# Order of weight preparation and accumulator banks at the seam between the last MLP and the token-mixing stage

## Chip, cores and metric

One core of one Trainium2 chip (TensorE = PE with its weight loads PEld, VectorE = DVE, ScalarE = ACT, GpSimd = POOL, SyncE = SP). The time is the device time of one execution in microseconds, the median over runs, as printed in the table below.

## What is computed

Four sequences of 768 tokens, 8 heads of 48, pass through three layers. The reference, cut to what matters:

```
# gated linear attention, per head:
state = f[t] * state + k[t] v[t]^T ;  y[t] = q[t] state         (f = sigmoid(f_logit))
# layer 2, x is [4, 768, 384]:
h = x^T @ U @ V ;  u = x + h^T
x = u + relu(u @ w_ch1) @ w_ch2                                  # 384 -> 1536 -> 384
# layer 3:
theta = x @ w_theta
y = w_tok_r @ (x * cos(theta)) + w_tok_i @ (x * sin(theta))      # 768 x 768 over tokens
u = x + y
out = u + relu(u @ w_ch)
```

## The kernel before

Activations lie with channels on the 128 partitions, so a batch is `xT[b]`, three blocks of 128 channels by 768 tokens. Every fp32 product is done with both operands split into a high and a low part (`split`: ACT copies the high part, L135, POOL subtracts for the low one, L132), as three products hi x hi, lo x hi, hi x lo. Weights come as 64-bit floats and are turned into fp32 on the chip (`fetch`): a DMA on the SP queue into a buffer of a ring, two ACT scalings (L863, L865: `scale`), two DVE instructions (L868, L871: `join`), then the split. So a piece of weights has four steps, called load, scale, join and store here. The ring for the weights of the last layer has four buffers; a buffer is free for the next load when POOL has done the subtraction of the piece that was in it.

The kernel has three stretches: attention of batch 0; three MLPs of layer 2 (batches 0 to 2) with the attention of the next batch laced in; the MLP of batch 3, called the last MLP, with the preparation of layer 3 laced in; then layer 3 for the four batches, called the next stage.

*The MLP* (`moe1`) goes in groups of four of the 12 blocks of hidden channels, for one half of the tokens after the other (six groups in the last MLP, 24 blocks in all). A piece is nine matmuls of 128 x 128 weights on 384 tokens. `w1g` (L477) forms a hidden block in bank A3 or A4; ACT takes the relu as high part hh (L482), DVE the low part hl (L483). `w2g` (L493 with hh, L496 with hl) adds it into three accumulators in banks A0, A1 and A2. When a group's last block is in, DVE adds the accumulators to `xT` (L500). The list alternates: w1g of block n, then w2g of block n - 1. The first six of the last MLP's 48 pieces go ahead of the stretch that this is about; 42 remain (`m3[6:]`).

*The next stage* works in units of 128 tokens, six to a batch, counted from 0. For a unit, `theta` has five parts: `prep` splits the 128 columns (POOL x2lo), `tr` transposes them into bank B1 (L586, ACT copies x2tok, L588), `mmt` multiplies by w_theta into bank B0 (nine matmuls, L598) and reduces the angle on DVE (kk and r, L602 to L606) and takes two sines on ACT (sh, sn, L609, L610), `trig` forms z = x cos, x sin on DVE (L619 to L622) and copies the high part zh on ACT (L623), `rest` subtracts the low part zl on POOL. `tok` has six pieces of six matmuls (L646) that add the unit's share into all six banks A0 to A5, in the order of the banks. The theta parts run two units ahead of `tok`: units 0 and 1 are prepared during the last MLP (a list called `pre`), unit n + 2 between the `tok` pieces of unit n. From the second batch on, the output product (`chan`, L674, banks B0 and B1) of the batch before is laced in too.

*The order.* The engines take instructions in program order, and the program's order is written by hand. Each list is of (cost, function) pairs. `merge` gives each item of a side list a place in a stretch of the main list by its cost, `place` by a position of its own: a step at position x of a main list stands ahead of the first piece whose middle lies behind x of the list's total cost. Before the change the weight pieces pass through `staged` and `tok_weights`: one item of a side list does the scaling of piece i + 1, the join of piece i, the store of piece i - 1 and the load of the piece three further on, all at one place. The six pieces of w_theta and w_ch lie by `CWA` in the first 0.3 of the last MLP, and 20 of the 30 items of the token weights' list by `M3` in the rest. The other ten are run one at a time, three in each unit of the next stage (`cv`). Loads of the token weights overwrite the tiles `W` of MLP weights that are no longer needed (`WMAP`).

## Time and profile before

| | us |
|---|---|
| median of 3 runs (lowest to highest) | 732.85 (732.4 to 736.12) |
| the profiled execution | 735.42 |
| its span from first to last instruction | 733.6 |
| PE busy in the span | 696.8 (95%) |
| DVE, ACT, POOL busy | 463.2 (63%), 290.2 (40%), 317.6 (43%) |

A profile row shows one execution. Times in it count from the start of the span. A row of a timeline may merge several instructions of one kind (x6); its second number is then their length together. PE's matmuls overlap, so the pitch from start to start says more than the length of one. "idle before <-" names what ended the idle time of the engine. An ACT, DVE or POOL row that waits holds up everything behind it on its engine.

### The profile page before, as it was taken

Reading aid. Unit: us, or ns where it says so; the run is one execution under the profiler, and the core shown is the slowest. Engines: PE = TensorE matmul, PEld = TensorE weight load, DVE = VectorE, ACT = ScalarE, POOL = GpSimd, SP = SyncE. Lnnn points to the kernel's source line nnn. Section 1 sums busy time; section 2 is a strip of 40 time slices with the busy share of each in tenths; the row PEclk is TensorE's granted clock in tenths of the full one; section 3 lists DMA queues with packets and bytes.
Section 4 is the critical chain, followed back from the end, with each engine's and each line's share of the span. In section 5 each row is a group of like instructions: output and inputs, shape, how many; then the busy total and the mean of one; then the engine's idle time right before and its main releaser. Section 6 shows DMA issues by size and latency. Waiting matters only on the chain.

```text
span 733.6 us, 12972 instructions
## 1 busy us (share of the span) xinstructions
PE 696.8 (95%) x5221; PEld 655.9 (89%) x5221; DVE 463.2 (63%) x705; ACT 290.2 (40%) x613; POOL 317.6 (43%) x338
## 2 busy tenths in 40 slices
PE   7988899999999999999999999898899999999996
PEld 6766798999899999899989999898799999999996
DVE  8795778666544545544433578779786569459433
ACT  1577474533332224333323466555442233233211
POOL 5586657542443333342432144335555245336212
PEclk9799899999999999999999999999899999999999
DMA  9795253322122222122000243333000000000102
GB/s 176 172 267 133 68 156 75 55 42 49 44 44 45 44 45 43 45 44 44 2 2 1 87 140 104 102 108 109 0 1 22 33 13 11 33 22 1 44 21 70
DMA packets 17956, 46.14 MB, mean 63 GB/s; under 512 B 2272, under 2 KB 8544, under 8 KB 17888
## 3 DMA queue, kind: packets, MB, share of 16 engines
q1 hardware_dynamic: 15760, 39.13, 21.7%
q10 hardware_dynamic: 2128, 6.10, 3.1%
q8 instruction: 43, 0.70, 0.4%
q14 instruction: 25, 0.20, 0.1%
HBM read 40.50 MB, written 4.72 MB: 62 GB/s over the span
## 4 chain that ended last, share of the span: by engine, by line
PE 39%; DVE 12%; ACT 4%; issue 2%; POOL 2%; DMA 1%; DVEq 0%; POOLq 0%; ACTq 0%
PE ps_A L646 12%; PE ps_A L477 7%; PE ps_B L674 5%; PE ps_A L493 5%; PE ps_B L598 3%; PE ps_A L496 2%; DVE r L606 1%; DVE r L605 1%; DVE kk L603 1%; DVE z L622 1%; DVE z L621 1%; DVE sh L619 1%; DVE r L604 1%; DVE kk L602 1%; DVE r L871 1%
## 5 line engine op out<-in xcount | busy, mean ns | idle before, releaser
L483 DVE SCALAR_TENSOR_TENSOR hl<-ps_A,hh 128x384 fp32r<-128x384 f32 x96 | 53.1, 554 | 151.5 <-ACT hh L482 151.3
L646 PE MATMUL ps_A<-W,zh 128*128 128x384 f32 x576 | 126.1, 340 | 4.2 <-ACT zh L623 3.9
L493 PE MATMUL ps_A<-hh,W 128*128 128x384 f32 x576 | 122.1, 347 | 4.1 <-DVE xT L500 2.9
L477 PE MATMUL ps_A<-uh,W 128*128 128x384 f32 x576 | 121.3, 345 | 1.7 <-ACT uh L444 1.7
L493 PEld LDWEIGHTS ps_A<-hh,W 128*128 128x128 f32 x576 | 100.5, 191 | 8.0 <-ACT r L865 2.9
L646 PEld LDWEIGHTS ps_A<-W,zh 128*128 128x128 f32 x576 | 101.1, 189 | 5.1 <-ACT zh L623 4.5
L477 PEld LDWEIGHTS ps_A<-uh,W 128*128 128x128 f32 x576 | 100.0, 190 | 4.8 <-ACT uh L444 2.5
L482 ACT ACTIVATE hh<-ps_A 128x384 fp32r<-128x384 f32 x96 | 46.9, 489 | 140.0 <-PE ps_A L477 139.1
L132 POOL TENSOR_TENSOR zl<-z,zh 128x768 fp32r<-128x768 f32 x24 | 44.8, 1866 | 102.1 <-ACT zh L623 92.6
L220 DVE RECIPROCAL f<-p 112x128 f32<-112x128 f32 x96 | 87.0, 930 | 0.7
L646 PE MATMUL ps_A<-W,zl 128*128 128x384 f32 x288 | 74.3, 339 | 1.9 <-POOL zl L132 1.9
L132 POOL TENSOR_TENSOR ul<-xT,uh 128x384 fp32r<-128x384 f32 x45 | 49.8, 1115 | 52.9 <-ACT uh L444 35.7
L223 POOL TENSOR_TENSOR raw<-raw,f 112x256 f32<-112x256 f32 x48 | 37.5, 782 | 76.4 <-DVE f L220 61.8
L477 PE MATMUL ps_A<-ul,W 128*128 128x384 f32 x288 | 66.9, 338 | 0.6 <-POOL ul L132 0.6
L496 PE MATMUL ps_A<-hl,W 128*128 128x384 f32 x288 | 66.0, 337 | 0.0
L213 POOL TENSOR_TENSOR raw<-raw,p 112x512 f32<-112x512 f32 x24 | 30.9, 1287 | 66.1 <-DVE p L209 54.1
L646 PEld LDWEIGHTS ps_A<-W,zl 128*128 128x128 f32 x288 | 52.5, 190 | 2.5 <-POOL zl L132 2.5
L477 PEld LDWEIGHTS ps_A<-ul,W 128*128 128x128 f32 x288 | 51.9, 189 | 1.6 <-POOL ul L132 1.6
L496 PEld LDWEIGHTS ps_A<-hl,W 128*128 128x128 f32 x288 | 52.0, 190 | 0.0
L609 ACT ACTIVATE sh<-r 128x384 f32<-128x384 f32 x24 | 12.6, 526 | 85.6 <-DVE r L606 85.6
L132 POOL TENSOR_TENSOR W<-r,W 128x384 fp32r<-128x384 f32 x24 | 27.5, 1148 | 42.0 <-ACT W L135 42.0
L602 DVE TENSOR_SCALAR kk<-ps_B 128x384 f32<-128x384 f32 x24 | 13.3, 554 | 43.7 <-PE ps_B L598 43.7
(161 smaller groups left out, 1255.2 us busy)
## 6 DMA issues: line engine op xcount, KB each, us to landing
raw<-in_qkf_dram SPq DMA_DIRECT2D x41, 288.0 KB, 5.2
r<-in_wtok_dram SPq DMA_DIRECT2D x24, 384.0 KB, 3.2
vt<-in_v_dram SPq DMA_DIRECT2D x24, 192.0 KB, 5.4
out_dram<-o SPq DMA_DIRECT2D x24, 192.0 KB, 1.9
xT<-in_w_dram SPq DMA_DIRECT2D x5, 768.0 KB, 4.8
w<-in_w_dram ACTq DMA_DIRECT2D x4, 768.0 KB, 6.9
w<-in_w_dram SPq DMA_DIRECT2D x2, 768.0 KB, 8.2
raw<-in_qkf_dram ACTq DMA_DIRECT2D x5, 288.0 KB, 5.6
```

The source lines that it names most:

```text
L132: eng.tensor_tensor(out=out_, in0=a, in1=b, op=ALU.subtract)
L213: nc.gpsimd.tensor_tensor(out=x, in0=x, in1=p, op=ALU.mult)
L220: nc.vector.reciprocal(out=f[:, j], in_=p[:, j])
L223: nc.gpsimd.tensor_tensor(out=x, in0=x, in1=f[:, j - 1:j + 1], op=ALU.mult)
L477: mm(out=t, lhsT=w1t(lo, fb)[:, k, 128 * fo:128 * fo + 128], rhs=x[:, k], start=(n == 0), stop=(n == 8))
L482: nc.scalar.activation(out=hh, in_=t, func=ACTF.Relu)
L483: nc.vector.scalar_tensor_tensor(out=hl, in0=t, scalar=0.0, in1=f32(hh), op0=ALU.max, op1=ALU.subtract)
L493: mm(out=st["acc"][k], lhsT=w2t(lo, fb)[:, fo, 128 * k:128 * k + 128], rhs=hh, start=(first_of(f) and lo == 0), stop=False)
L496: mm(out=st["acc"][k], lhsT=w2t(0, fb)[:, fo, 128 * k:128 * k + 128], rhs=hl, start=False, stop=last_of(f))
L598: mm(out=t, lhsT=x[:, k], rhs=w[:, k], start=(n == 0), stop=(n == 8))
L646: mm(out=t, lhsT=z[:, i, 128 * k:128 * k + 128], rhs=w[:, S * i + HT * th:S * i + HT * th + HT], start=(s == 0 and n == 0), stop=(s == NCH ...
L674: mm(out=t, lhsT=w[:, k, 128 * m:128 * m + 128], rhs=x[:, k], start=(n == 0), stop=(n == 8))
```

## The change

In the last MLP, the groups' accumulators alternate between banks A0, A1, A2 and banks A5, B0, A2, and the adds into `xT` go in the order A2 first. The theta products of the first two units use bank B1. The 30 pieces of the last layer's weights (w_theta, w_ch, token weights, in this order) get a ring of four tiles, and each of their four steps gets a position of its own, in `NPOS`: below 1.0 in the last MLP, above 1.0 in the first batch of the next stage. The 11 parts of the theta list for units 0 to 2 get positions too (`PPOS`). `place` puts them into the two lists. `staged`, `tok_weights`, `cv` and the constants of their lanes go.

```diff
--- before.py
+++ after.py
@@ -33,9 +33,39 @@
 WARM = 28
 KEEP = (15, 1, 1, 1, 1, 1, 0, 3, 16, 0)
 NPRE = 6
-N3 = 20
-CWA = 0.101
-M3 = ((0.333, 0.867), (0.3, 0.999))
+NPOS = (
+    (0.0241, 0.0644, 0.0738, 0.0988),
+    (0.0327, 0.1266, 0.1466, 0.1716),
+    (0.0387, 0.0965, 0.1019, 0.1953),
+    (0.1482, 0.1974, 0.1982, 0.257),
+    (0.1717, 0.2209, 0.2217, 0.2574),
+    (0.2218, 0.2763, 0.2771, 0.3021),
+    (0.1961, 0.2721, 0.2921, 0.3444),
+    (0.2578, 0.3057, 0.3257, 0.3448),
+    (0.2686, 0.3245, 0.3378, 0.4217),
+    (0.3157, 0.3892, 0.4092, 0.4392),
+    (0.3464, 0.4224, 0.4402, 0.4629),
+    (0.4081, 0.4783, 0.504, 0.5388),
+    (0.4758, 0.5558, 0.5758, 0.6037),
+    (0.4694, 0.5765, 0.5881, 0.6181),
+    (0.5027, 0.5727, 0.5927, 0.659),
+    (0.5472, 0.6172, 0.6372, 0.7129),
+    (0.6045, 0.66, 0.6639, 0.7498),
+    (0.6206, 0.664, 0.684, 0.7502),
+    (0.6796, 0.7552, 0.7696, 0.9267),
+    (0.7599, 0.7662, 0.8484, 0.9399),
+    (0.7555, 0.8704, 0.8712, 0.9403),
+    (0.8292, 0.8974, 0.9192, 0.9746),
+    (0.9315, 0.9828, 0.9928, 1.022),
+    (0.9407, 0.9937, 1.004, 1.124),
+    (0.9525, 0.9978, 1.008, 1.188),
+    (1.001, 1.002, 1.096, 1.205),
+    (1.047, 1.07, 1.12, 1.412),
+    (1.126, 1.206, 1.256, 1.412),
+    (1.269, 1.369, 1.419, 1.525),
+    (1.33, 1.361, 1.48, 1.64),
+)
+PPOS = (0.3588, 0.3882, 0.428, 0.4924, 0.4929, 0.5759, 0.5869, 0.7626, 0.7666, 0.8224, 0.8643)
 W0 = (100, 1200, 800, 600)
 
@@ -486,7 +516,8 @@
         def w2g(th, f):
             hh, hl = st.pop(("h", th, f))
             if first_of(f):
-                st["acc"] = [ps(f"A{k}", [128, HT]) for k in range(NK)]
+                two = b == B - 1 and order.index((th, f)) % 2
+                st["acc"] = [ps(t, [128, HT]) for t in (("A5", "B0", "A2") if two else ("A0", "A1", "A2"))]
             fb, fo = divmod(f, 4)
             for k in range(NK):
                 for lo in range(2):
@@ -495,10 +526,12 @@
             for k in range(NK):
                 mm(out=st["acc"][k], lhsT=w2t(0, fb)[:, fo, 128 * k:128 * k + 128], rhs=hl,
                    start=False, stop=last_of(f))
-                if last_of(f):
+            if last_of(f):
+                for k in (2, 0, 1) if b == B - 1 else range(NK):
                     u = xT[b][:, k, HT * th:HT * th + HT]
                     nc.vector.tensor_tensor(out=u, in0=st["acc"][k], in1=u, op=ALU.add)
 
+        order = [(th, o) for o in range(0, NF, span) for th in range(2)]
         todo = [(th, f) for o in range(0, NF, span) for th in range(2) for f in range(o, o + span)]
         for n, a in enumerate(todo):
             L.append((1470, lambda a=a: w1g(*a)))
@@ -511,63 +544,43 @@
     thw = {}
 
     def weights_2(pool):
-        L = []
-
-        def issue(nm, src, i):
+
+        ring = [pool.tile([128, 768], I32, name=f"r64_{i}") for i in range(4)]
+
+        def issue(n, src):
+            return fetch(nc, pool, src, [128, 384], nc.sync, buf=ring[n % 4])
+
+        def dst(nm, i):
+            if nm in ("th", "ch"):
+                if i == 0:
+                    thw[nm] = [pool.tile([128, NK, DM], F32R, name=nm + x) for x in ("hi", "lo")]
+                return [t[:, i] for t in thw[nm]]
             if i == 0:
-                thw[nm] = (pool.tile([128, NK, DM], F32R, name=nm + "hi"), pool.tile([128, NK, DM], F32R, name=nm + "lo"))
-            return fetch(nc, pool, src[:, 384 * i:384 * i + 384], [128, 384], nc.sync, "r64", bufs=4)
+                st["tok", nm] = [wtile(k) for k in WMAP[nm]]
+            return [t[:, 384 * i:384 * i + 384] for t in st["tok", nm]]
 
         def store(nm, i, w):
-            hi, lo = thw[nm]
-            split(hi[:, i], lo[:, i], w, lo_eng=nc.gpsimd)
-
-        for nm, src in (("th", wth), ("ch", wch)):
-            for i in range(NK):
-                L.append((lambda nm=nm, src=src, i=i: issue(nm, src, i), lambda w, nm=nm, i=i: store(nm, i, w)))
-        return staged(L, 4)
-
-    def staged(L, ahead, delay=1, lag=1):
-
-        got, out = {}, [(0, lambda i=i: got.update({i: L[i][0]()})) for i in range(min(ahead, len(L)))]
-
-        def step(i):
-            if i + 1 < len(L):
-                got[i + 1][0]()
-            if i < len(L):
+            split(*dst(nm, i), w, lo_eng=nc.gpsimd)
+
+        tok_ = [(s, i, wtok[s]) for s in range(NCH) for i in range(4)]
+        order = [("th", i, wth) for i in range(NK)] + [("ch", i, wch) for i in range(NK)] + tok_
+        return steps_of([(lambda n=n, src=src, i=i: issue(n, src[:, 384 * i:384 * i + 384]),
+                          lambda w, nm=nm, i=i: store(nm, i, w)) for n, (nm, i, src) in enumerate(order)])
+
+    def steps_of(L):
+
+        got = {}
+
+        def one(i):
+            def load():
+                got[i] = L[i][0]()
+
+            def join():
                 got[i] = got[i][1]()
-            if i >= lag:
-                L[i - lag][1](got.pop(i - lag))
-            j = i - max(lag, delay) + ahead
-            if i >= max(lag, delay) and j < len(L):
-                got[j] = L[j][0]()
-
-        out.append((0, lambda: got[0][0]()))
-        out += [(1000, lambda i=i: step(i)) for i in range(len(L) + lag)]
-        return out
-
-    def tok_weights(pool):
-        L = []
-        ring = []
-
-        def issue(n):
-            if n == 0:
-                ring.extend(pool.tile([128, 384, 2], I32, tag="r64", bufs=4, name="r64") for _ in range(4))
-            s, i = divmod(n, 4)
-            return fetch(nc, pool, wtok[s, :, 384 * i:384 * i + 384], [128, 384], nc.sync,
-                         buf=ring[n % 4].rearrange("p n t -> p (n t)"))
-
-        def store(n, w):
-            s, i = divmod(n, 4)
-            if i == 0:
-                st["tok", s] = wtile(WMAP[s][0]), wtile(WMAP[s][1])
-            hi, lo = st["tok", s]
-            sl = slice(384 * i, 384 * i + 384)
-            split(hi[:, sl], lo[:, sl], w, lo_eng=nc.gpsimd)
-
-        for n in range(4 * NCH):
-            L.append((lambda n=n: issue(n), lambda w, n=n: store(n, w)))
-        return staged(L, 4, lag=1)
+
+            return load, lambda: got[i][0](), join, lambda: L[i][1](got.pop(i))
+
+        return [one(i) for i in range(len(L))]
 
     WMAP = {0: (6, 7), 1: (0, 1), 2: (8, 9), 3: (2, 3), 4: (10, 11), 5: (4, 5)}
 
@@ -591,7 +604,7 @@
         def mmt():
             hi, lo = st.pop(("x2", b, s))
             wh, wl = thw["th"]
-            t = ps("B0", [128, DM])
+            t = ps("B0" if (b, s) > (0, 1) else "B1", [128, DM])
             n = 0
             for (x, w) in ((hi, wh), (hi, wl), (lo, wh)):
                 for k in range(NK):
@@ -791,40 +804,25 @@
         p2 = fast.enter_context(tc.tile_pool(name="st2", bufs=1))
         units = [(b, s) for b in range(B) for s in range(NCH)]
         th = [theta(p2, *u) for u in units]
-        pre = [(330, th[0][0]), (330, th[0][1]), (1470, th[0][2]), (500, th[0][3]), (900, th[0][4]),
-               (330, th[1][0]), (330, th[1][1]), (1470, th[1][2]), (500, th[1][3]), (900, th[1][4]),
-               (0, th[2][0])]
-        tw = tok_weights(p2)
-        cw = weights_2(p2)
-        merge(m3[6:], (0.0, 0.0, cw[:4]), (CWA, 0.3, cw[4:]), (*M3[0], pre), (*M3[1], tw[:N3]))
-        tw = tw[N3:]
+        pre = [th[0][0], th[0][1], th[0][2], th[0][3], th[0][4], th[1][0], th[1][1], th[1][2], th[1][3], th[1][4], th[2][0]]
+        timed = [list(zip(PPOS, pre)), []]
+        for fs, at in zip(weights_2(p2), NPOS):
+            for f, x in zip(fs, at):
+                timed[x >= 1.0].append((x % 1.0, f))
+        place(m3[6:], timed[0])
         nop = lambda: None
+        main = []
         for n, (b, s) in enumerate(units):
             _, tr, mmt, trig, rest = th[n + 2] if n + 2 < len(units) else [nop] * 5
             prep = th[n + 3][0] if n + 3 < len(units) else nop
             cl = [f for _, f in chan(p2, b - 1)[2 * s - 2:2 * s]] if b and s in (1, 2, 3) else [nop] * 2
             tk = [f for _, f in tok(b, s)]
-
-            def cv():
-                run(tw[:1])
-                del tw[:1]
-
-            tk[0]()
-            prep()
-            tr()
-            cv()
-            tk[1]()
-            mmt()
-            cv()
-            tk[2]()
-            cl[0]()
-            tk[3]()
-            cv()
-            trig()
-            tk[4]()
-            cl[1]()
-            rest()
-            tk[5]()
+            fs = (tk[0], prep, tr, tk[1], mmt, tk[2], cl[0], tk[3], trig, tk[4], cl[1], rest, tk[5])
+            main += [(980 if f in tk else 0, f) for f in fs]
+            if n == NCH - 1:
+                place(main, timed[1])
+                main = []
+        run(main)
         run(chan(p2, B - 1))
     fast.close()
```

## Rows read from the trace of the kernel before

**Rows 1.** The page's strip of 40 slices of the span: granted TensorE clock in tenths.
```profile
PEclk9799899999999999999999999999899999999999
```

**Rows 2.** Table of stretches: start:end, length, busy us of each engine (instructions), clock, DMA.
```profile
408.44:485.24 76.80, 72.44 (x404) 70.08 (x402) 57.16 (x100) 45.80 (x98) 30.30 (x27) 0.98 0.41 119
485.24:509.80 24.56, 24.56 (x144) 24.30 (x144) 19.78 (x31) 12.07 (x26) 10.59 (x9) 1.00 0.35 95
509.80:535.80 26.00, 20.27 (x98) 18.99 (x98) 21.03 (x32) 10.87 (x23) 13.57 (x10) 0.87 0.06 18
```

**Rows 3.** Waits of PE, 405 to 540 us: total us, times, longest.
```profile
PE ps_A L646 <- ACT zh L623: 3.9, 2, 2.4
PE ps_A L493 <- DVE xT L500: 2.9, 2, 2.6
PE ps_A L646 <- POOL zl L132: 1.9, 2, 0.9
```

**Rows 4.** Timeline of PE in the last MLP: start, us, operation, idle before and its releaser.
```profile
408.44 1.29 PE L493 MATMUL ps_A<-hh,W 128*128 128x384 f32 x6
...
410.09 1.20 PE L477 MATMUL ps_A<-uh,W 128*128 128x384 f32 x6
...
411.65 1.20 PE L493 MATMUL ps_A<-hh,W 128*128 128x384 f32 x6
...
428.49 1.46 PE L493 MATMUL ps_A<-hh,W 128*128 128x384 f32 x6 [1.08 <-ACT chhi L135]
...
473.99 2.26 PE L493 MATMUL ps_A<-hh,W 128*128 128x384 f32 x6 [2.58 <-DVE xT L500]
...
485.24 0.96 PE L646 MATMUL ps_A<-W,zh 128*128 128x384 f32 x4 [0.30 <-DVE xT L500]
```

**Rows 5.** Timeline of ACT ahead of the longest hole.
```profile
470.28 0.85 ACT L623 ACTIVATE zh<-z 128x768 fp32r<-128x768 f32 x1 [2.71 <-DVE z L622]
...
472.32 0.47 ACT L482 ACTIVATE hh<-ps_A 128x384 fp32r<-128x384 f32 x1
```

**Rows 6.** Timeline of DVE at the same place.
```profile
472.82 0.56 DVE L483 SCALAR_TENSOR_TENSOR hl<-ps_A,hh 128x384 fp32r<-128x384 f32 x1 [1.51 <-ACT hh L482]
473.30 1.48 DVE L500 TENSOR_TENSOR xT<-ps_A,xT 128x384 f32<-128x384 f32 x3
```

**Rows 7.** Timeline of PE in the next stage: first pieces of units 1 to 5.
```profile
493.50 0.85 PE L646 MATMUL ps_A<-W,zh 128*128 128x384 f32 x4
...
501.67 0.85 PE L646 MATMUL ps_A<-W,zh 128*128 128x384 f32 x4
...
511.43 0.98 PE L646 MATMUL ps_A<-W,zh 128*128 128x384 f32 x4 [1.47 <-ACT zh L623]
...
523.49 0.96 PE L646 MATMUL ps_A<-W,zh 128*128 128x384 f32 x4 [2.38 <-ACT zh L623]
...
535.80 0.85 PE L646 MATMUL ps_A<-W,zh 128*128 128x384 f32 x4
```

**Rows 8.** Timeline of DVE in the next stage.
```profile
489.54 0.56 DVE L602 TENSOR_SCALAR kk<-ps_B 128x384 f32<-128x384 f32 x1 [2.37 <-PE ps_B L598]
...
494.55 1.34 DVE L871 SCALAR_TENSOR_TENSOR r<-r 128x384 int32<-128x384 int32 x1
...
498.04 0.55 DVE L622 TENSOR_TENSOR z<-sn,x2tok 128x384 f32<-128x384 f32 x1
...
522.00 0.55 DVE L622 TENSOR_TENSOR z<-sn,x2tok 128x384 f32<-128x384 f32 x1
...
529.09 0.55 DVE L622 TENSOR_TENSOR z<-sn,x2tok 128x384 f32<-128x384 f32 x1
```

**Rows 9.** Second instruction of the join, all of the kernel: duration ns min/median/max.
```profile
L871 DVE SCALAR_TENSOR_TENSOR r<-r x24: 559/560/2084, 433.8 to 518.4; 128x384 int32<-128x384 int32 x24
```

**Rows 10.** Timeline of POOL beside the stretched join.
```profile
494.44 1.03 POOL L132 TENSOR_TENSOR W<-r,W 128x384 fp32r<-128x384 f32 x1 [4.62 <-ACT W L135]
```

**Rows 11.** The page's DMA issues: KB each, median us from issue to landing.
```profile
r<-in_wtok_dram SPq DMA_DIRECT2D x24, 384.0 KB, 3.2
```

## The prediction

> **What bounds the kernel now.** I began with the page's strip of forty slices: the granted TensorE clock is full nearly everywhere; of its three dents two belong to the kernel's start (slices 2 and 5), the third is slice 29, 513 to 532 us [rows 1], just behind the last MLP. The table of stretches says what they are worth: in the last MLP (408.44 to 485.24 us, 76.80 us) PE is busy for 72.44 us, in the first half of the next stage for all of 24.56 us, in the next 26.00 us for only 20.27 us at a clock of 0.87 [rows 2]. So PE is the bound everywhere, and what can be won is the time that it does not work at full pace in these two stretches. The waits of PE there name three releasers: the ACT copy zh of the trigonometric unit (3.9 us), the evacuation of an accumulator (2.9) and POOL's zl (1.9) [rows 3].
>
> What the holes cost in full, clock and restart included, comes from the pitch. In the MLP a piece of nine matmuls starts every 1.56 us (410.09, 411.65) [rows 4]. The stretch holds 42 such pieces and two theta products of nine matmuls: 44 x 1.56 = 68.64 us. In the next stage an undisturbed unit takes 501.67 - 493.50 = 8.17 us [rows 7]; six pieces of six matmuls (1.04 each by the same pitch) and a theta product make 7.80, so the transposes are 0.37, and two sets of them 0.74. The MLP's excess is then 76.80 - 68.64 - 0.74 = **7.4 us**. In stage two (units counted from 0) unit 5 starts at 535.80 [rows 7]; five units from 485.24 would bring it at 526.09: an excess of **9.7 us**. No change of order can win more than these 17.1 us.
>
> Why PE waits. At 473.99 it had stood for 2.58 us [rows 4]; hh of two pieces before was done only at 472.32 + 0.47, because ACT works in order and zh ended at 471.13 just ahead of it with two scalings and a split between them [rows 5]; hl followed at 472.82, the accumulator's add at 473.30 [rows 6]. The six matmuls that follow took 2.26 us, where undisturbed ones take 1.20 [rows 4]: a half-speed stretch behind the hole. The hole at 428.49 (1.08 us) has the same form, an ACT split of a weight piece ahead of hh, itself waiting for the join on DVE [rows 4]. In stage two DVE sets the pace: z of one unit ends every (522.00 - 498.04)/2 = 12.0 us while three joins stand in each unit, but 529.09 - 522.00 = 7.1 us after the last join [rows 8]. PE's unit is 8.17, so the lead is eaten and units 3 and 4 stand for 1.47 and 2.38 us at their start and more behind it [rows 7].
>
> **The change, part by part.** *Work.* Pieces, instructions and DMAs stay as they are: 30 pieces, each one 384 KB load, two ACT scalings, two DVE instructions of the join, one ACT split, one POOL subtraction. Counting the positions, 23 joins now lie in the MLP's program (pieces 0 to 22), 21 before, and 7 in stage two, 9 before. *Two more joins in the MLP* cost DVE 2 x 2 x 0.56 us at the median, 2 x 2 x 2.08 at the longest row of that instruction [rows 9]: 2.2 to 8.3 us of DVE, beside an engine with 76.80 - 57.16 = 19.6 us free there [rows 2]; I take nothing on PE for it, since a join is on PE's path only where hl stands behind it (below).
>
> *Stage two.* With three joins a unit costs 12.0 us and with none 7.1: 1.6 a join, POOL's blocking included [rows 8]. In the new order joins 22 to 24 stand ahead of the first theta chain of the stage, 25 between it and the trigonometry, 26 behind, then one in unit 1 and two in unit 2. From the stage's start T: three adds 1.5 [rows 6], three joins of 1.2 to 1.6 (to T + 5.1 to 6.3; the theta product is ready near T + 4.3, as kk in the old trace at 489.54, behind an idle 2.37) [rows 8]. From kk to the end of z it was 498.59 - 489.54 = 9.05 with two joins; with one 7.5: z of unit 2 at T + 12.6 to 13.8, zh 0.85 later [rows 5], and PE wants it at T + 16.3, two units on. Unit 3: join 26, join 27 and 7.1: T + 22.1 to 24.1, zh to 24.9, wanted at T + 24.5. Unit 4: one join and 7.1: 30.4 to 32.8, zh to 33.7, wanted at 32.7. So at the low price nothing is late, at the high one about 1 us. I take 0.6 us left of 9.7, with 0 and 3 as ends (3: a hole of 1 us at each of units 2 to 4). **Gain 9.1** (6.7 to 9.7). What is late next then is the end of the batch, which the change leaves alone.
>
> *Accumulators.* Groups now take A0, A1, A2 and A5, B0, A2 in turn, and A2 is added first. So the first two thirds of the next group's first six matmuls need no add, and the third needs one. Price: the add's wait in front of a group goes, except where A2's add is over 0.7 us (four of nine matmuls of 1.56) late. At the end, the first piece of stage two writes A0, free for long: the 0.30 at 485.24 goes [rows 4]. The theta product that uses B0 comes after two pieces and the transposes, some 2.4 us in, the three adds take 1.5. The products of units 0 and 1 move to B1, which the transposes of the same unit use: they wait for ACT's copy x2tok, placed more than one piece earlier; nothing, or 0.5 us if ACT is that late.
>
> But alternation alone would not have emptied the largest hole: hh came at 472.79 and the add at 473.30 + 0.5, so about 1.2 us of it is the add, the rest is ACT's order. *That order stays in one place.* By the new positions the theta product of unit 1 and its trigonometry stand at 0.7626 and 0.7666, both ahead of the same piece. From kk to the end of z it is 9.05 us with two joins [rows 8], 5.9 to 6.7 without them; with 0.85 for zh, 0.47 for hh [rows 5] and 0.3 of hand-overs that hh comes 7.5 to 8.3 us after the product. PE has four pieces, 6.24 us, before it needs it. And between sn and zh there now stands the scaling of piece 19, whose load is queued on SP behind that of piece 20, which waits for the slot of piece 16; landing takes 3.2 us [rows 11]. So a hole of 1.3 us at least, 4.2 at worst (today's: 2.58, the 1.06 of slow matmuls, the slow ones behind them) [rows 4]; I take 2.0, near the low end, since nothing but the load is worse placed than the chain I added up. A second such place is the theta chain of unit 0 with joins 9 and 10 around it ahead of A2's add: 0 to 1.5, I take 0.5. The hole at 428.49 goes: there joins are now placed two pieces ahead of their splits, and no load is fresh. **MLP gain 7.4 - 2.5 = 4.9** (1.7 to 6.1).
>
> *Loads.* Each step has its own place, so a load is issued as soon as its slot is free; ring depth and count are unchanged, nothing on the path. For the other batches the adds only move in program text, each still waiting for its own matmul: nothing.
>
> **Sum.** 9.1 + 4.9 = 14.0 us. The profiled execution took 735.42 us: 721.4. It is 2.57 above the median of the runs, 732.85; the same gain from the median gives 718.9. The holes, and the slow matmuls behind them above all, may be a little larger in the slower execution; I put **720.0**.
>
> **Port.** A join beside a POOL subtraction is stretched: at 494.55 the second instruction took 1.34 us [rows 8], the subtraction ran from 494.44 for 1.03 [rows 10], and it takes 0.56 otherwise [rows 9]. The Trainium skill, page "SBUF — State Buffer", section "Who interferes with whom", says that a VectorE instruction with two SBUF inputs and a GpSimd instruction that reads SBUF exclude one another for their whole length; the row agrees. If each of the 23 joins lost one subtraction so, that is the rival "serial" below.
>
> **Rivals.** A measurement of this kernel can tell about 0.5% (3.7 us) from no change.
> - *Half of it* (0.21): only one stretch is relieved. For it: the trigonometry's order stays ahead of hh, and z of units 3 and 4 has no slack at the high price. MLP alone 727.9 from the median, stage two alone 723.8.
> - *Moved, not removed* (0.11): what stage two gives up, the MLP loses, since two joins more stand in front of hl there; hl's lag is unseen where it is covered. 730 to 735. Against it: DVE's 19.6 us free.
> - *Serial* (0.06), the side of slower: DVE and POOL exclude one another so often that they set PE's pace. In the three stretches DVE and POOL are busy for 57.16 + 30.30 + 19.78 + 10.59 + 21.03 + 13.57 = 152.4 us, the stretches last 127.4 [rows 2]: 25.0 us of them overlap. With z and hl on their path throughout, the time grows by as much as overlap is lost: past 3.7 us lost it is slower, and at two fifths lost (10 us) it is 743. For it: joins are packed in pairs in the MLP now. Against: hl and the adds read PSUM, and PE keeps its pace through most of the MLP today beside the same POOL work.
> - *Forecast* (0.62).
>
> **Numbers.** Range 715 to 729: the low end is all 17.1 us from the median (715.8) and 0.8 of rounding in the excesses, the high end takes in the half case; left out are "moved", "serial" and the ends, about 2 in 10. Faster by over 0.5% (below 729.2): 0.62 + 0.21 = 0.83; the same 0.11; slower 0.06.
>
> **What would show it.** Right: no hole ahead of the first piece of stage two, z about every 8.2 us from the first unit on, full clock up to the batch's end, unit 5 some 9 us earlier behind the MLP's end; one hole of 1 to 2 us left in the MLP's last third, ended by hh behind zh. Wrong: holes ended by zh in units 2 to 4, hl late in pieces with joins 13 to 20, or an excess of over 5 us left in the MLP.

## The result and the profile after

The changed kernel takes **726.72 us** (median of 4 runs, 726.1 to 727.49) against 734.13 us for the kernel before on the same chip (4 runs): a ratio of 0.9901 with an interval of 0.9873 to 0.9929. It is faster by 7.4 us, where 12.85 were forecast (732.85 to 720.0); the sign and the range held. The profiled execution of the changed kernel took 727.49 us, 7.93 less than that of before.

The page's engine line and its strip of the clock, of the changed kernel:

```profile
PE 693.4 (96%) x5221; PEld 653.4 (90%) x5221; DVE 461.0 (64%) x705; ACT 290.8 (40%) x613; POOL 318.7 (44%) x338
PEclk9799899999999999999999999999999999999999
```

The dent in slice 29 [rows 1] is gone, and each engine runs as many instructions as before (5221, 705, 613 and 338). The table of stretches (columns as in [rows 2]): the last MLP, the next stage up to unit 5, and from there to the first output product.

```profile
407.98:482.63 74.65, 72.14 (x404) 70.79 (x403) 56.03 (x100) 46.38 (x99) 32.29 (x28) 0.98 0.39 123
482.63:525.06 42.43, 41.29 (x242) 40.48 (x241) 37.80 (x59) 22.27 (x46) 19.53 (x16) 1.00 0.21 65
525.06:549.94 24.88, 22.09 (x127) 20.94 (x127) 22.87 (x34) 10.21 (x21) 16.73 (x14) 1.00 0.00 1
```

In the trace of before the same three are 76.80, 50.56 (485.24 to 535.80) and 22.21 us (535.80 to 558.01, its first output product). So the MLP gave 2.15 us, the stage up to unit 5 gave 8.13, and **the end of the batch took 2.67 back**. With 0.46 ahead of the MLP and a remainder of -0.14 for all that lies behind the output product that is 2.15 + 8.13 - 2.67 + 0.46 - 0.14 = 7.93, the whole difference.

PE's waits from 405 to 555 us (as in [rows 3]):

```profile
PE ps_A L659 <- POOL zl L162: 1.9, 3, 0.8
PE ps_A L524 <- ACT hh L512: 1.5, 1, 1.5
PE ps_B L687 <- ACT x2tok L601: 1.4, 1, 1.4
PE ps_A L524 <- DVE xT L532: 1.0, 2, 0.7
PE ps_A L659 <- DVE xT L665: 0.7, 1, 0.7
```

The waits for zh (3.9 us) are gone; those for the adds fell from 2.9 to 1.0. PE's timeline in the MLP, answering to [rows 4]:

```profile
442.77 0.62 PE L524 MATMUL ps_A<-hh,W 128*128 128x384 f32 x2 [0.73 <-DVE xT L532]
...
456.14 0.62 PE L524 MATMUL ps_A<-hh,W 128*128 128x384 f32 x2 [0.25 <-DVE xT L532]
...
471.22 0.62 PE L524 MATMUL ps_A<-hh,W 128*128 128x384 f32 x2 [1.46 <-ACT hh L512]
...
473.84 2.12 PE L507 MATMUL ps_A<-uh,W 128*128 128x384 f32 x6
```

Three holes are left, and they hold the stretch's excess over the pitch. By the forecast's own count, 68.64 us of pieces and 0.74 of transposes, that is 74.65 - 69.38 = 5.3 us. By the starts of the pieces around them the first costs 1.03 us, the second 0.53, and the third 3.67, because matmuls behind it ran slowly (2.12 us for six, where [rows 4] have 1.20).

ACT ahead of the third hole ([rows 5]), and DVE ahead of the first ([rows 6]):

```profile
469.07 0.57 ACT L861 ACTIVATE r<-r 128x384 f32<-128x384 f32 x1 [1.53 <-DMA r<-in_wtok_dram]
...
469.95 0.84 ACT L636 ACTIVATE zh<-z 128x768 fp32r<-128x768 f32 x1
470.69 0.86 ACT L512 ACTIVATE hh<-ps_A 128x384 fp32r<-128x384 f32 x2
```

```profile
441.10 0.55 DVE L866 SCALAR_TENSOR_TENSOR r<-r 128x384 int32<-128x384 int32 x1
441.69 0.56 DVE L869 SCALAR_TENSOR_TENSOR r<-r 128x384 int32<-128x384 int32 x1
442.16 1.48 DVE L532 TENSOR_TENSOR xT<-ps_A,xT 128x384 f32<-128x384 f32 x3
```

Both are places that the forecast named. On ACT the scaling of piece 19 waits 1.53 us for its load, zh stands behind it, and hh behind zh. On DVE the theta chain of unit 0 and a join stand ahead of the adds, of which A2's ends first, but too late.

PE in the next stage ([rows 7]):

```profile
482.63 0.85 PE L659 MATMUL ps_A<-W,zh 128*128 128x384 f32 x4
...
508.66 0.62 PE L659 MATMUL ps_A<-W,zl 128*128 128x384 f32 x2 [0.72 <-POOL zl L162]
...
517.49 0.62 PE L659 MATMUL ps_A<-W,zl 128*128 128x384 f32 x2 [0.42 <-POOL zl L162]
...
540.14 0.97 PE L659 MATMUL ps_A<-W,zh 128*128 128x384 f32 x4 [0.66 <-DVE xT L665]
...
543.96 0.62 PE L659 MATMUL ps_A<-W,zl 128*128 128x384 f32 x2 [0.76 <-POOL zl L162]
...
549.94 0.79 PE L687 MATMUL ps_B<-uh,chhi 128*128 128x384 f32 x3 [1.37 <-ACT x2tok L601]
```

The 0.30 us ahead of the stage's first piece is gone, units 2 to 4 stand for 0.72 + 0.42 = 1.14 us, all of it for zl, and around the batch's end, from 540.14 on, stand three holes, of which two were not there before and the third, now 1.37 us, was 0.73.

**The lead of z** says why. I call so the time from the end of a unit's z (DVE) to that unit's start on PE. The start is taken from the transposes that stand in the unit behind its first piece, less the 1.04 us of that piece. DVE's z of units 6 and 7, then the transposes that stand in the same units, in the changed kernel:

```profile
529.30 0.55 DVE L635 TENSOR_TENSOR z<-sn,x2tok 128x384 f32<-128x384 f32 x1
538.25 1.36 DVE L635 TENSOR_TENSOR z<-sn,x2tok 128x384 f32<-128x384 f32 x1
```

```profile
534.28 0.49 PE L599 MATMUL ps_B<-ident,xT 128*128 128x128 f32 x3
544.42 0.49 PE L599 MATMUL ps_B<-ident,xT 128*128 128x128 f32 x3
```

and the same z in the kernel before:

```profile
537.32 0.55 DVE L622 TENSOR_TENSOR z<-sn,x2tok 128x384 f32<-128x384 f32 x1
546.30 1.37 DVE L622 TENSOR_TENSOR z<-sn,x2tok 128x384 f32<-128x384 f32 x1
```

From the end of one z to the next it takes DVE 539.61 - 529.85 = 9.76 us in the changed kernel, without idle time. Before it took 547.67 - 537.87 = 9.80, of which DVE stood for 1.00 waiting for PE's theta product: 8.8 of work, since the adds of the batch into `xT` lie in its queue there. PE's unit is 8.17, so at the batch's end a lead is spent in either kernel. Before, the holes at units 3 and 4 had let DVE get ahead, and unit 6 began with a lead of 6.07 (transposes at 544.98); after, with 534.28 - 1.04 - 529.85 = 3.39, and its pitch became 544.42 - 534.28 = 10.14 instead of 8.15. The lead at unit 7 fell from 4.42 to 3.77 and its pitch grew by as much, from 12.28 to 12.94. 1.99 + 0.66 = 2.65 of the 2.67 us.

z of units 2 to 5 ends at 495.03, 505.80, 514.63 and 522.71. The first interval is 10.77 us; then z comes after 8.83 and 8.08. The forecast's sign was 8.2 from the first unit on, and before it was 12.0 [rows 8].

### The profile page after: what moved, and what is told of

Its sections match the earlier page's. It is cut to its first block, busy times and chain, and to the rows that moved or that the text cites. A ratio compares the mean times of both kernels' runs of the same rounds, so it can differ in the third digit from the quotient of the medians.

```text
span 725.7 us, 12964 instructions
## 1 busy us (share of the span) xinstructions
PE 693.4 (96%) x5221; PEld 653.4 (90%) x5221; DVE 461.0 (64%) x705; ACT 290.8 (40%) x613; POOL 318.7 (44%) x338
## 4 chain that ended last, share of the span: by engine, by line
PE 34%; DVE 12%; issue 4%; DMA 3%; POOL 2%; ACT 2%; SPq 0%; POOLq 0%; DVEq 0%; ACTq 0%
PE ps_A L659 10%; PE ps_A L507 7%; PE ps_B L687 5%; PE ps_A L524 4%; PE ps_B L611 2%; DMA r<-in_wtok_dram 2%; PE ps_A L527 2%; DVE r L618 2%; DVE kk L616 1%; DVE r L619 1%; POOL W L162 1%; DVE z L634 1%; DVE z L635 1%; DVE xT L665 1%; DVE sh L632 1%
## 5 line engine op out<-in xcount | busy, mean ns | idle before, releaser
L524 PE MATMUL ps_A<-hh,W 128*128 128x384 f32 x552 | 118.3, 344 | 2.5 <-ACT hh L512 1.5
L524 PEld LDWEIGHTS ps_A<-hh,W 128*128 128x128 f32 x552 | 95.6, 189 | 5.8 <-DVE xT L532 2.0
L527 PEld LDWEIGHTS ps_A<-hl,W 128*128 128x128 f32 x276 | 49.8, 189 | 0.0
L622 ACT ACTIVATE sh<-r 128x384 f32<-128x384 f32 x24 | 12.6, 526 | 77.4 <-DVE r L619 77.4
L162 POOL TENSOR_TENSOR W<-r,W 128x384 fp32r<-128x384 f32 x24 | 26.8, 1130 | 30.4 <-ACT W L165 28.8
L636 ACT ACTIVATE zh<-z 128x768 fp32r<-128x768 f32 x24 | 20.3, 847 | 45.2 <-DVE z L635 45.2
```

The source lines that it names most:

```text
L162: eng.tensor_tensor(out=out_, in0=a, in1=b, op=ALU.subtract)
L524: mm(out=st["acc"][k], lhsT=w2t(lo, fb)[:, fo, 128 * k:128 * k + 128], rhs=hh, start=(first_of(f) and lo == 0), stop=False)
L527: mm(out=st["acc"][k], lhsT=w2t(0, fb)[:, fo, 128 * k:128 * k + 128], rhs=hl, start=False, stop=last_of(f))
L636: nc.scalar.activation(out=zh, in_=z, func=ACTF.Copy)
```

## The experiments

Two theories. *Order*: the positions carry the gain, and what is missing is two named queues (ACT and DVE in the MLP) and DVE's place in the next stage; put each step elsewhere, and the rest comes. *Pace*: over the whole seam DVE, stretched by POOL, is the bound behind PE's back, so that a hole that is closed in one place opens in another, and only less work gives time. The start of the MLP, ahead of which all kernels are alike, lies anywhere from 405.2 to 410.0 us in the traces, so I read the two stretches: the MLP, and the next stage up to its first output product (72.77 us before). Each stretch is of one profiled execution, while the time is the median of the runs, with their number behind it. The kernels ran on several chips, so a ratio is to runs of the kernel before on the same chip (its medians there: 732.45 to 734.13), and kernels are compared by it. The profiled execution of before took 735.42 us, 1.3 above its median, so what a stretch gained against it is read a little too high.

| kernel | MLP | next stage | sum | time (runs) | ratio to before |
|---|---|---|---|---|---|
| before | 76.80 | 72.77 | 149.57 | 734.13 (4) | |
| after | 74.65 | 67.31 | 141.96 | 726.72 (4) | 0.9901 [0.9873, 0.9929] |
| 1: piece 19's scaling later | 72.15 | 68.17 | 140.32 | 726.97 (1) | |
| 2: trigonometry later | 74.20 | 67.96 | 142.16 | 724.82 (1) | |
| 3: both | 71.53 | 67.30 | 138.83 | 725.87 (9) | 0.9897 [0.9859, 0.9935] |
| 4: last joins spread | 75.00 | 71.84 | 146.84 | 731.92 (10) | 0.9975 [0.9957, 0.9994] |
| 5: last seven joins left out | 72.53 | 64.56 | 137.09 | 720.51 (1) | |
| 6: before with the banks | 74.82 | 71.93 | 146.75 | 733.65 (10) | 0.9983 [0.9961, 1.0005] |
| 7: after without the banks | 75.67 | 66.15 | 141.82 | 727.77 (7) | 0.9924 [0.9900, 0.9949] |
| 8: joins behind the trigonometry | 74.67 | 67.91 | 142.58 | 729.68 (1) | |
| 9: all edits together | 74.20 | 66.34 | 140.54 | 726.75 (4) | 0.9892 [0.9858, 0.9926] |
| 10: eight of POOL's subtractions left out | 73.25 | 63.88 | 137.13 | 720.33 (1) | |
| 11: after, again | 72.37 | 67.52 | 139.89 | 725.58 (5) | 0.9899 [0.9868, 0.9929] |
| 12: kernel 3, stores and loads earlier | 73.68 | 66.37 | 140.05 | 724.84 (4) | 0.9885 [0.9858, 0.9913] |

### The third hole of the MLP: 1, 2 and 3

```diff
-    (0.7599, 0.7662, 0.8484, 0.9399),
+    (0.7599, 0.803, 0.8484, 0.9399),
```

> One position changes: the scaling of piece 19 goes from 0.7662 to 0.803, two pieces later, behind hh of block 20. In the changed kernel ACT waited 1.53 us for that piece's load ahead of zh of unit 1, and w2g of block 20 and the piece behind it cost 3.7 us more than their pitch (1.46 us of idle, then slow matmuls). Load theory: the fresh load is all of it; hh comes in time, the two pieces cost under 0.3 us more than the pitch, the MLP stretch shrinks from 74.65 to about 71.2 us. Order theory: z itself ends at 469.24, so zh and hh still come late; hh 0.7 us earlier, 0.7 to 0.9 us of idle stay, the slow matmuls may go: the stretch shrinks by 0.7 (clock still falls) to 2.7 us.

The same step of `PPOS`, for the second kernel:

```diff
-PPOS = (0.3588, 0.3882, 0.428, 0.4924, 0.4929, 0.5759, 0.5869, 0.7626, 0.7666, 0.8224, 0.8643)
+PPOS = (0.3588, 0.3882, 0.428, 0.4924, 0.4929, 0.5759, 0.5869, 0.7626, 0.8, 0.8224, 0.8643)
```

> One position changes: the trigonometry of unit 1 goes from 0.7666 to 0.800, two pieces later, behind hh of block 20; the scaling of piece 19 stays ahead of it. Order theory (zh ahead of hh is all of it): no idle ahead of w2g of block 20, stretch about 71.2 us. Load theory: ACT still waits for the load ahead of hh, hh some 0.7 us earlier than before, 0.4 to 0.9 us of idle stay. If both hold, each of the two single moves leaves 0.4 to 0.9 us and the stretch lies between 72 and 74 us in both.

Both edits in one:

> Both positions move (scaling of piece 19 to 0.803, trigonometry of unit 1 to 0.800). If the two causes together make the hole: none is left there, the MLP stretch is 71.2 us (74.65 less 3.5), and the time about 723.2 (726.7 less 3.5). Rival: the next stage takes it back, since zl of unit 1 and join 18 come later: the stretch shrinks but the time stays above 725.

PE's timeline at this place, of the first, the second and the third kernel:

```profile
471.85 0.61 PE L524 MATMUL ps_A<-hh,W 128*128 128x384 f32 x2 [0.60 <-ACT hh L512]
```

```profile
467.51 0.62 PE L524 MATMUL ps_A<-hh,W 128*128 128x384 f32 x2 [0.87 <-ACT hh L512]
...
470.56 0.62 PE L524 MATMUL ps_A<-hh,W 128*128 128x384 f32 x2 [2.08 <-DVE xT L532]
```

```profile
470.74 0.62 PE L524 MATMUL ps_A<-hh,W 128*128 128x384 f32 x2 [0.21 <-DVE xT L532]
```

and ACT in the third:

```profile
467.16 0.47 ACT L512 ACTIVATE hh<-ps_A 128x384 fp32r<-128x384 f32 x1
470.25 0.84 ACT L636 ACTIVATE zh<-z 128x768 fp32r<-128x768 f32 x1 [2.62 <-DVE z L635]
```

With only the scaling moved 0.60 us is left, with only the trigonometry moved 0.87 and a new hole of 2.08 in front of the group's adds, where the moved chain now stands; with both, hh is done at 467.63 and the hole is 0.21. So the hole has the two causes that the forecast gave it. Each is shown against the kernel with both edits (0.60 to 0.21, and 0.87 to 0.21), since the hole of the changed kernel itself was 1.46 us in one execution and 0.98 in another (below). The MLP of 71.53 is the shortest of all, and the next stage did not take it back (67.30). The time, though, is not resolved from that of the changed kernel (0.9897 against 0.9901): nine runs lie between 723.03 and 730.54 us, further apart than the edit is worth.

### What the banks carry: 6 and 7

Kernel 6 is before with only the three edits of the banks, the order of the adds and B1; kernel 7 is after with these taken back:

```diff
...
-                two = b == B - 1 and order.index((th, f)) % 2
-                st["acc"] = [ps(t, [128, HT]) for t in (("A5", "B0", "A2") if two else ("A0", "A1", "A2"))]
+                st["acc"] = [ps(f"A{k}", [128, HT]) for k in range(NK)]
...
```

> The kernel before with the alternating banks, the order of adds and bank B1 for the first two theta products, all positions as before. By the prediction's working the banks alone take 1.2 us off the largest hole, 0.3 off each of the two small ones, perhaps the slow matmuls: the MLP stretch shrinks from 76.80 by 1.5 to 3 us, stage two keeps its 9.7 us of excess, time 731 to 732.5. Rival: the banks carry the MLP's part: stretch at or under the changed kernel's 74.65.

> The changed kernel with the banks of before (A0, A1, A2 for every group, adds in the order 0, 1, 2, each theta product in B0), all new positions kept. If the positions carry the gain: the next stage keeps it, the MLP stretch grows by 1 to 3 us over 74.65 (each group's first pieces wait for three adds, and at its end A0 waits for its add, 0.3), time 728 to 730. Rival: the banks matter little once the order is new: within 0.7 us of 726.7. Other rival: without them the MLP loses all that it won: 76.8 and more, and slow matmuls.

Banks alone took 76.80 - 74.82 = 1.98 us off the MLP, and the next stage did not grow (71.93 against 72.77). The time still cannot be told from that of before; its interval reaches down to 0.9961, or 2.9 us, so it does not contradict the trace either. Positions alone are worth a ratio of 0.9924. PE's waits in kernel 7, in the MLP:

```profile
PE ps_A L523 <- DVE xT L530: 4.4, 3, 1.5
```

Without the second set of banks a hole of about 1.5 us stands ahead of each of three groups. The MLP is 1.0 to 3.3 us longer than in the two traces of the changed kernel, and yet the next stage is 1.2 to 1.4 us shorter. In those holes DVE got ahead with its queue: z of unit 2 ends 11.24 us behind the stage's start, against 12.40 and 12.61. The sums, 141.82 against 141.96 and 139.89, hardly differ. With the new positions the rival "moved, not removed" is thus in part right, for the banks.

### Where the last joins stand: 4, 5 and 8

```diff
-    (1.001, 1.002, 1.096, 1.205),
-    (1.047, 1.07, 1.12, 1.412),
-    (1.126, 1.206, 1.256, 1.412),
-    (1.269, 1.369, 1.419, 1.525),
-    (1.33, 1.361, 1.48, 1.64),
+    (1.001, 1.002, 1.13, 1.205),
+    (1.047, 1.07, 1.29, 1.45),
+    (1.126, 1.206, 1.455, 1.6),
+    (1.269, 1.369, 1.62, 1.7),
+    (1.33, 1.361, 1.79, 1.83),
```

> In the next stage joins 25 to 29 move: each stands behind a unit's trigonometry instead of between its theta chain and its trigonometry, one to a unit (1.13, 1.29, 1.455, 1.62, 1.79), with the stores behind them. Number of joins unchanged. Lead theory: the joins ate the lead of z over PE (6.2 us at unit 5 in the kernel before, 2.4 in the changed one), and without a lead the batch's end, where DVE also adds six accumulators, costs PE 3.6 us instead of 0.9. Then z of unit 5 is 4 us or more ahead, PE's idle at the batch's end falls to about 1.5, the time falls by 2 to 3.5 us. Rival: the lead is lost to the joins however they lie, since DVE has no idle time in these units; within 0.7 us of the changed kernel.

PE in unit 5 of this kernel:

```profile
528.03 0.44 PE L659 MATMUL ps_A<-W,zh 128*128 128x384 f32 x1 [1.82 <-POOL W L162]
...
532.57 0.69 PE L659 MATMUL ps_A<-W,zh 128*128 128x384 f32 x1 [3.08 <-ACT W L165]
...
534.67 0.69 PE L659 MATMUL ps_A<-W,zh 128*128 128x384 f32 x1 [1.41 <-POOL W L162]
```

I had put the stores so late that PE waits 6.3 us for the weights W of unit 5 themselves. It says nothing against spreading the joins, and was tried again with earlier stores: joins 25, 27 and 28 go behind the trigonometry of their unit, 29 one unit on.

```diff
+    (1.001, 1.002, 1.125, 1.205),
+    (1.047, 1.07, 1.135, 1.412),
+    (1.126, 1.206, 1.29, 1.412),
+    (1.269, 1.369, 1.455, 1.525),
+    (1.33, 1.361, 1.62, 1.68),
```

> The changed kernel with joins 25, 27, 28 of the next stage behind the trigonometry of their unit instead of ahead of it, 26 behind 25, and join 29 one unit later (store at 1.68). Same number of joins, stores else where they were, so that no token weight comes late. Lead theory (what costs is a join between theta chain and z): z of units 2 to 4 ends 1.2 us or more earlier, the waits of 0.97 and 0.67 us over the pitch at units 2 and 3 go, the lead at unit 6 grows from 3.4 to 4.5 us or more, and the batch's end gives back about 1: from the stage's start to the first output product 64.5 to 65.5 us against 67.31. Rival (DVE has no idle time there, so the place of a join does not matter): 66.7 to 67.9.

The stage took 67.91 us, not shorter than 67.31: here a join costs no less behind the trigonometry than ahead of it. DVE has little idle time to put it into: from the stage's start to the end of z of unit 6 it is busy for 41.82 of 47.22 us, and 2.0 us of the rest is the wait for the MLP's last product. Unit 6 began with a lead of 2.39 and its pitch was 11.11. Leaving the joins of pieces 23 to 29 out shows the whole price (`ring_` is the ring's four tiles; with `raw` the store takes the piece as it lies there):

```diff
...
+            def raw():
+                got[i] = ring_[i % 4][:, 0:768].rearrange("p (n t) -> p n t", t=2)[:, :, 0].bitcast(F32)
...
-            return load, lambda: got[i][0](), join, lambda: L[i][1](got.pop(i))
+            return load, lambda: got[i][0](), (raw if i >= 23 else join), lambda: L[i][1](got.pop(i))
```

> The changed kernel without the joins of pieces 23 to 29 (the two DVE instructions that put the fp32 value together are left out for these pieces, so their part of the token weights is not computed; loads, scalings, stores stay). Lead theory: DVE gains 7 x 1.2 to 1.6 us; z of unit 5 ends 5 us or more ahead of its use, units 2 to 4 show no waits, the batch's end costs PE about 1 us instead of 3.6; in all 3 to 4.5 us shorter than the changed kernel's 727.5. Rival: the batch's end costs what it costs by its own adds and subtractions; then only the 1.5 us of excess in units 0 to 4 go.

67.31 - 64.56 = 2.75 us of the stage, with a lead of 4.45 at unit 6 and a pitch of 9.08.

### The changed kernel again, and all edits at once: 11 and 9

> The changed kernel as it is, as the measure for e8 and e9 on the same chip: 725 to 728 us, MLP stretch 74 to 75.5 us, next stage to the first output product 67 to 68. If the slow matmuls behind the third hole are a matter of chance, the stretch may lie at 72.5 to 73.

```profile
469.14 0.62 PE L524 MATMUL ps_A<-hh,W 128*128 128x384 f32 x2 [0.98 <-ACT hh L512]
...
471.18 1.20 PE L507 MATMUL ps_A<-uh,W 128*128 128x384 f32 x6
```

In this trace of the same kernel the third hole is 0.98 us, and the six matmuls behind it take 1.20 again, not 2.12. The MLP is 72.37, so 4.4 us shorter than before's: 2.3 us of the MLP's result differ between two executions of one kernel, most of it at and behind this hole.

Kernel 9 has the edits of 3, joins 27 to 29 as in 8, joins 22, 23 and 25 earlier, the joins in front of late adds moved behind them, and stores 18 to 21 with the loads behind them earlier, for instance:

```diff
-    (0.6796, 0.7552, 0.7696, 0.9267),
+    (0.6796, 0.7552, 0.7696, 0.799),
```

> A version made from what the runs showed: both moves of e3; join 10 and join 14 behind a group's adds instead of ahead of them; stores 18 to 21 earlier by 2 to 5 pieces (0.799 to 0.945), so that loads 22 to 25 come earlier and joins 22 and 23 fit into DVE's idle time in the MLP's last three pieces; joins 26 to 29 behind a unit's trigonometry. If the holes have the causes that I name: MLP stretch 69.5 to 70.3 us (pitch alone 69.4; 74.65 in the changed kernel, 71.53 in e3), next stage to the first output product 64 to 65.5 us (67.31), in all 7 us less than the changed kernel in these two stretches, time 718 to 721. Rival: each hole closed opens the next one, since DVE and POOL together set the pace: sum of the two stretches not under 137.5 us (141.96 in the changed kernel, 138.83 in e3).

```profile
472.83 0.61 PE L524 MATMUL ps_A<-hh,W 128*128 128x384 f32 x2 [1.63 <-DVE xT L532]
...
486.55 0.79 PE L611 MATMUL ps_B<-thhi,x2hi 128*128 128x384 f32 x3 [0.80 <-DVE xT L532]
```

The holes stand in other places, and the sum is no better than that of kernel 3. In the next stage that is what the pace theory expects. For the MLP it is not shown: there DVE is busy for only 56.03 of 74.65 us in the changed kernel, kernel 3 came within 2.2 us of the pitch (71.53 - 69.38), and a better order of that stretch may exist.

### Is it POOL behind DVE: 10, and 12

In kernel 10 POOL's subtraction of the last eight pieces goes, ACT writing zeros in its place; DVE's work is whole.

```diff
-            split(*dst(nm, i), w, lo_eng=nc.gpsimd)
+            hi, lo = dst(nm, i)
+            if isinstance(nm, int) and 4 * nm + i >= 16:
+                nc.scalar.activation(out=hi, in_=w, func=ACTF.Copy)
+                nc.scalar.activation(out=lo, in_=w, func=ACTF.Copy, scale=0.0)
+            else:
+                split(hi, lo, w, lo_eng=nc.gpsimd)
```

> The changed kernel without POOL's subtraction for the eight pieces stored in the next stage (22 to 29): their low parts are set to zero by ACT instead (one copy of 0.45 us each), so this part of the split product is left out. Joins and positions stay. Exclusion theory (DVE instructions wait out POOL's subtractions, and this eats the lead of z): DVE instructions of 0.36 and 0.56 us that took 1.0 to 1.7 us are fewer, z of units 2 to 4 earlier by about 1 us each, waits at units 2 and 3 under half (from 1.6 us to under 0.8), lead at unit 6 over 4.2 us (3.4), from the stage's start to the first output product under 66 us (67.3 and 67.5 in the two traces of the changed kernel). Rival (only DVE's own instructions count): 67 to 68.

The next stage up to the first output product in the table of stretches, after and then kernel 10:

```profile
482.63:549.94 67.31, 63.39 (x367) 61.42 (x367) 60.67 (x92) 32.48 (x67) 36.26 (x29) 1.00 0.14 41
```

```profile
478.96:542.84 63.88, 62.52 (x367) 61.62 (x366) 56.67 (x92) 35.90 (x75) 27.16 (x21) 1.00 0.13 43
```

Two of DVE's groups by line in the same stretches, in the same order (busy us, mean ns of one, idle before; L871 and L624 are the changed kernel's L866 and L619):

```profile
L619 DVE TENSOR_SCALAR r<-r 128x384 f32<-128x384 f32 x7 | 6.7, 959 | 0.2
L866 DVE SCALAR_TENSOR_TENSOR r<-r 128x384 int32<-128x384 int32 x8 | 5.2, 655 | 2.0 <-ACT r L863 2.0
```

```profile
L624 DVE TENSOR_SCALAR r<-r 128x384 f32<-128x384 f32 x7 | 5.3, 756 | 0.2
...
L871 DVE SCALAR_TENSOR_TENSOR r<-r 128x384 int32<-128x384 int32 x8 | 4.4, 554 | 2.3 <-ACT r L868 2.3
```

PE waits for nothing that the profile shows from the stage's start to 542.84, its first output product, and the stage falls from 67.31 to 63.88. DVE does the same 92 instructions in 56.67 us instead of 60.67: the same join instruction takes 554 instead of 655 ns, the reduction's last 756 instead of 959. So POOL's subtractions had stretched DVE's instructions by 4.0 us. Two other ways in which POOL could have held PE up do not explain it: DVE's wait for a scaled piece did not get shorter when the buffers were freed without POOL (2.3 us against 2.0), and at units 3 and 4 of the changed kernel POOL stood idle for 3.97 and 1.84 us waiting for zh before it began the late zl. Eight subtractions of POOL less give the stage 67.31 - 63.88 = 3.43 us, more than seven joins of DVE less. L619 has one tile operand, not two as the join has. At the batch's end of the changed kernel a row of its kind took 1.60 us (531.29, L616) while POOL's zl ran from 530.82 for 1.85; at the same place before it took 0.36 (540.57, L603). The Trainium skill, page "SBUF — State Buffer", section "Who interferes with whom", names `tensor_scalar` too among the VectorE operations that can hold the pair of ports which GpSimd shares; the rows agree, and the forecast had named the joins alone.

The last kernel keeps all the work: kernel 3, with stores 18 to 21, 23 and 24 and loads 22 to 25 earlier.

> e3 with the stores of pieces 18 to 21 earlier (0.84 to 0.95 instead of 0.927 to 0.975) and so loads 22 to 25 too (0.846 to 0.955), joins where they were. Aim: DVE's waits for fresh scalings at the start of the next stage (0.55 and 0.54 us) go, z of unit 2 comes 1 us earlier. If so: MLP stretch 71.3 to 72 us, next stage to the first output product 66 to 66.5, sum 137.5 to 138.5 (138.83 in e3, 141.96 and 139.89 in the two traces of the changed kernel), time 723 to 725. Rival: the subtractions of these four pieces, now in the MLP's last third, block hl there: stretch over 72.5, sum over 139.5.

```profile
443.99 0.62 PE L524 MATMUL ps_A<-hh,W 128*128 128x384 f32 x2 [1.64 <-DVE xT L532]
```

The next stage gained 0.9 us over kernel 3 (66.37), and the MLP lost 2.2 (73.68). One hole is the edit's, for hl (0.75, at 481.16): subtractions now stand there, and the join ahead of hl takes 0.94 and 1.28 us beside them. The other is not: the hole ahead of a group's adds shown here was 0.72 us in kernel 3, and every step that this edit moved stands far behind it, at 0.84 of the MLP or later. At that place the second instruction of a join and a subtraction on POOL begin within 0.1 us of each other. In kernel 3 DVE is first, and POOL's row is stretched; in kernel 12 POOL is first, and DVE's is:

```profile
437.76 0.56 DVE L869 SCALAR_TENSOR_TENSOR r<-r 128x384 int32<-128x384 int32 x1
437.85 1.37 POOL L162 TENSOR_TENSOR W<-r,W 128x384 fp32r<-128x384 f32 x1 [0.54 <-ACT W L165]
```

```profile
438.05 1.04 POOL L162 TENSOR_TENSOR W<-r,W 128x384 fp32r<-128x384 f32 x1 [0.36 <-ACT W L165]
438.13 1.37 DVE L869 SCALAR_TENSOR_TENSOR r<-r 128x384 int32<-128x384 int32 x1
```

These 0.81 us of DVE are most of the 1.1 us by which the adds, counted from the MLP's start, came later in kernel 12. So which of the two starts first, by 0.1 us, moved a hole of PE by 0.9. Without that the sum would be about 140.05 - 0.92 = 139.1, still not under kernel 3's. Kernel 12's ratio is the lowest of the kernels that compute everything, 0.9885, but its interval overlaps those of the changed kernel and of kernel 3. No version here is shown to beat the changed kernel.

The batch's end over these kernels (us). The sum of the lead at unit 6 and its pitch stays at 13.5 wherever PE waits there (in kernels 1, 2, 3, 7, 9 and 12 too it is 13.52 to 13.54):

| kernel | lead at unit 6 | pitch of unit 6 | sum |
|---|---|---|---|
| before | 6.07 | 8.15 | (no wait) |
| after, and again | 3.39, 3.40 | 10.14, 10.14 | 13.53, 13.54 |
| 5 | 4.45 | 9.08 | 13.53 |
| 6 | 5.68 | 8.16 | (no wait) |
| 8 | 2.39 | 11.11 | 13.50 |
| 10 | 5.14 | 8.41 | 13.55 |

So a unit-6 lead of 13.53 - 8.16 = 5.4 us costs nothing, and each us below it costs one.

## Why the prediction was right or wrong

**Right: the sign, and where the gain comes from.** Forecast 14.0 us of profiled time, got 7.93. It came from both stretches, which the rival "half of it" excludes, though the time lies within that rival's: 8.13 us from stage two (forecast 9.1, range 6.7 to 9.7) and 2.15 from the MLP (forecast 4.9, range 1.7 to 6.1). Kernels 6 and 7 show that the positions carry it. A granted clock of 1.00 in the next stage up to the batch's end, no hole at the stage's first piece, no hole ended by zh there, no wait for hl, and the one hole in the MLP's last third with hh behind zh were seen as written.

**The stage up to unit 5: right.** The sum for DVE holds: z of units 2, 3 and 4 ends 12.40, 23.17 and 32.00 us behind the stage's start, where 12.6 to 13.8, 22.1 to 24.1 and 30.4 to 32.8 were worked out. Still 1.6 us are left where 0.6 was taken, because the forecast asked only when zh is wanted. PE wants zl four matmuls (0.7 us) after zh, and POOL's subtraction, which makes it, takes 1.84 us (506.77 to 508.61, ahead of the hole that ends at 508.66). So the waits moved from zh to zl at units 3 and 4.

**The step that failed: "What is late next then is the end of the batch, which the change leaves alone".** It was priced at nothing and cost 2.67 us, 44% of what is missing (14.0 - 7.93 = 6.07). The code at the batch's end is the same, but what arrives there is not. The forecast reckoned whether z of units 2 to 4 is in time, and took being in time for enough. In the trace of before DVE comes out of the slow units with 6.07 us of lead at unit 6, made while PE stood; the changed kernel, in which z is only just in time, has a lead of 2.28 to 2.35 us at units 3 to 5, and of 3.39 at unit 6. The batch's end then needs 9.76 us of DVE in a unit, and takes it. The interval of 9.80, 8.8 of it work, stood in the trace of before, beside a pitch of 8.17.

**Mis-sized: the MLP, by 2.75 us** in the profiled execution, by 0.5 in the second trace (76.80 - 72.37 = 4.4). One of the forecast's signs of being wrong, over 5 us of excess left in the MLP, was so met in the first trace (5.3 us) and not in the second (72.37 - 69.38 = 3.0). The theta chain of unit 0 ahead of A2's add, taken at 0.5, measured 1.03. The third hole, taken at 2.0, measured 3.67: its idle time, 1.46, was near the low end of 1.3 that was worked out, and its two causes are shown by kernels 1 to 3, but the slow matmuls behind it made the rest, and they come in one trace of the same kernel and not in the other. Which of the two a run gets the forecast could not tell. The hole of 0.25 at 456.14 (0.53 in all) was not foreseen.

**Alternation alone**, taken at about 1.2 us of the largest hole and the 0.30 at the stage's start: 1.98 off the MLP in kernel 6. What the forecast did not see is that with the new positions the next stage gives back what the banks give the MLP (kernel 7); with the old ones it did not (kernel 6).

**Moved, not removed** was set at 0.11 for the time, and the time is not there. As a mechanism it is what limits the gain in the next stage: the holes of PE were DVE's slack. DVE is busy there for 60.56 of 72.77 us before and for 60.67 of 67.31 after, nearly the same work (93 and 92 instructions) with about half the idle time. **Serial**, the rival on the slow side, did not come: its price is real (kernel 10, 3.4 us in one stage) but was paid before the change as well (the stretched join of [rows 8]). The 25.0 us of overlap worked out for it are the least that the busy times allow, not the overlap itself. That DVE and POOL together set the pace of the next stage is shown where work was left out (5 and 10), and order alone did not shorten it by more than about 1 us (8, 9, 12). A cure that keeps all the work, with some of the low parts made on another engine, was not tried; ACT stands idle for half of the stage (20.2 of 42.43 us), but it is in the chain of zh.

## What to carry to other kernels

When an engine that runs ahead of PE is close to PE's own pace, don't ask only whether its result is in time in the stretch that changes; follow its lead through to the next place where it is slower than PE, because a hole that is closed takes lead away from there. An edit of order pays as long as some engine has idle time to take the moved step; in the next stage here DVE had little left, the holes came back elsewhere, and what helped was less work, on DVE or on the engine that stretches DVE's instructions. Read the gain of such an edit over all stretches up to the point where the lead has recovered, not at the hole.

## What the runs showed of the hardware that was not expected

An idle time of PE does not have one price. After 1.46 us of idle in the changed kernel the granted clock of the stretch from 467 to 478 us was 0.84, and six matmuls took 2.12 us that take 1.20 where it is 1.00; behind 1.80 in kernel 6, 1.82 in kernel 8 and 2.10 in kernel 4 it was 0.84 as well. After 1.46 in kernel 7, 1.60 in kernel 10, 1.63 in kernel 9 and 2.08 in kernel 2 it was 1.00 in a stretch of the same length around the hole. The two stretches, after and after again:

```profile
467.00:478.00 11.00, 9.46 (x44) 8.82 (x44) 8.02 (x17) 5.74 (x14) 2.81 (x2) 0.84 0.21 80
```

```profile
465.00:476.00 11.00, 9.95 (x56) 9.30 (x55) 9.55 (x18) 7.16 (x16) 3.98 (x4) 1.00 0.21 81
```

What decides it was not tried.

When an instruction of DVE and one of POOL that exclude each other begin almost together, the one that is 0.1 us earlier keeps its time and the other is stretched, in either direction (0.56 and 1.37 us in kernel 3, 1.37 and 1.04 in kernel 12).

A subtraction on POOL is not only as dear as POOL's own row: eight of them less, of 1.13 us each (10.1 us for 9) on an engine for which PE waits in three short holes, shortened a stage of 67.3 us by 3.4, because DVE's instructions beside them took 4.0 us less.
